# Linear attention and MLP on one core: finest level of the first two tiles by ScalarE and GpSimd, states by scans, no products of zeros in the first tile, and another order

## The chip, the cores and the metric

The kernel runs on one core of a Trainium2 chip. The metric is device time in microseconds (us), lower is better. All data is float32 except what is named otherwise. PE is the matrix engine (TensorE), PEld its weight loads, DVE VectorE, ACT ScalarE, POOL GpSimd, and SP SyncE, which issues most DMAs.

## The reference

```
state = 0                                   # B=4, H=8, S=768, D=48
for t in range(S):                          # linear attention with decay (RWKV6)
    cur   = outer(u * k[t], v[t])
    y[t]  = r[t] @ (state + cur)
    state = w[t][:, None] * state + outer(k[t], v[t])
x = y as (B*S = 3072 tokens, H*D = 384)
h = x @ w_in                                # 384 x 2048
g = 0.5 * h * (1 + erf(h / sqrt(2)))
out = g @ w_out                             # 2048 x 384
```

## The kernel before

**Tiles.** The work is cut into eight tiles, x = 0 to 7: four batches, two halves of T = 384 steps each. A tile has four pairs of heads (NP = 4), two heads of a pair lying on the two halves of the 128 partitions. The steps of a tile are cut into NC = 6 chunks of C = 64. Even tiles begin a batch with a state of zeros; odd tiles go on from the last state of the tile before.

**Attention of one tile.** Inside a chunk, the matrix of r times decay times k is built by levels. At level h (1, 2, 4, 8, 16, 32) PE multiplies r and k with the decays up to that distance in them (`products`, line 452), a part of the result is copied from PSUM into `a_sb`, and DVE multiplies r and k with the decays of the next level (lines 494 and 505). Tiles 0 and 1 do these six levels (`halves`); tiles 2 to 7 use a scheme of quarters. The copies of `halves` are masked DVE copies for h = 1, 2, 4, 8 (line 516) and plain ACT copies of blocks for h = 16 and 32 (line 513). The diagonal, with u in it, is a product of its own and one masked DVE copy (line 465). Then k is transposed (line 685, copied by ACT in line 687), PE makes each chunk's sum of k times v (`kv_ps`, line 711), and DVE chains the states of the six chunks: one `scalar_tensor_tensor` per chunk and pair (line 726), plus one copy per unit for the first chunk (line 731). PE adds up y inside the chunks (line 752) and y from the states (line 797), whose stationary operand is 64 contiguous columns of a state. DVE's `fence` (lines 762, 764) stands between the two groups of products. ACT and DVE copy y to `xT` (lines 804, 820), partly by way of `ysb` (line 823) and DMAs.

**MLP of one tile.** `mlp(x - 1)` is run on PE beside attention(x). Tile 0's MLP is plain (line 1059 first, h = x @ w_in in 128x384 steps); the later ones use sums of halves of the operands to save products (lines 929 and 1073, 128x192 steps). The gelu is on ACT (line 961 and its like). w_in and w_out come in 16 pieces that three ACT and two DVE instructions convert (lines 333, 334, 336; 345, 349) during tiles 0 and 1.

**Order.** Every engine runs its instructions in the order of the program. That order is written out by hand: `PLAN[x]` is a string, each character of which runs one step of a stream. In tile 0, `.` and `s` are two units of the attention (heads 0 to 3, heads 4 to 7), `l` loads and transforms, `c` the weight conversion, `f` the first steps of the next tile, `x` three products of zeros. In later tiles, `.` is the MLP of the tile before, `s` the attention, `f` the next tile's first steps.

**Products of zeros.** `keep_warm(n)` issues n matmuls of 128x512 bf16 zeros: 8 at the start, 2 behind each of 12 products of tile 0, and 6 ahead of the first MLP product.

**PSUM.** The products take pairs of banks; tiles 0 and 1 have three pairs, and two single banks serve the MLP.

Of the kernel before, what the change touches and what calls it, by code (L numbers as in the profile page):

```python
# [36 lines left out]
NC_SP = 8  # L37
HALFWAY = 2
PLAN = {
    0: "l.s....llsl.lssslslss.lc.l.slslls...ssss..lcs.s.s.l.ss..ss..sccs.c.s.llpssslw..cs.ffpcc",  # L40
    1: (
        "..ccswccc.csl.scscs.s.sccwsc.clccs.ccsccc.csc.lscclswwclc.scs.wcssw.ss.cclcsc.ccs.lclccsc."
        "ccclfccccccfccfcccccfccfccwf.ff......fw.sl.w.x.wx...x..x...xww"
    ),
    2: (
        "s.s.....ss....ssw.ws.wl.wsss.wws.s..lsl...lws.w..s.ww....s.s..l..sss.lssss....s..s..s.sls."
        "llsf.sf.fs..fl.xx.x.fxx"
    ),
    3: (
        "ls.ls....lss..ss.....ss..l.s.lsss.sss.s.s.s.ss..sss..sssssss....s.s..l...s..l.sslslsf.ffs."  # L50
        "..x.lx..xxx"
    ),
    4: (
        "lls.s.sss..s.l.........ssss.....sss.s.ss.s..s.sllss...s.s..l.sss.ss..s.ss...s..sslsll.s..f"
        ".sf.sf..ff..xx.xflxx"
    ),
    5: (
        "..ss...s..ssl....sls...s.sss..sss..sss.sls...sllss..sssss.s..l..s.s...s.slll..s.ssfsf.fsf."
        "....xxx.lxx"
    ),  # L60
    6: (
        "ss..sss...s.....s.sl..s...l.s.ssls.s.s..s..sssssl......ss.ssss.sl.sl...s.....ss..llsssl.f."
        "s.fsf.f.f.xx.l.xffxx"
    ),
    7: "....ss.s...s.s.s....s.sss..ss.ss.sss..s..sss..sssssss......s.s....s..ssss.s...x.x..xxx",
}


# [5 lines left out]
def kernel(  # L74
# [149 lines left out]
        for _ in range(n):  # L224
            nc.tensor.matmul(t, lhsT=zeros[:, 0:128], rhs=zeros, start=True, stop=True)

    keep_warm(8)


    masks = {h: const.tile([128, C // 2], U8, name=f"mask{h}") for h in LEVELS if h < 16}  # L230
# [122 lines left out]
    def attention(x, unit):  # L353
# [53 lines left out]
        for h in LEVELS:  # L407
            nb = n_u // (2 * h)
            t2 = tot[h].rearrange("p (n two) -> p n two", two=2)
            tot[2 * h] = tot_sb[:, at_tot:at_tot + nb]  # L410
            nc.vector.tensor_mul(tot[2 * h], t2[:, :, 0], t2[:, :, 1])
            at_tot += nb
            if x >= 2 and h == 2:
                yield
# [27 lines left out]
        else:  # L442
            yield

        def products(bs, right, width, rest=False):
            d = pair("d")
            n = 0
            for b in bs:
                for i in range(NI):
                    for g in range(2):  # L450
                        for p in range(2):
                            nc.tensor.matmul(d[half[p], g, n * width:(n + 1) * width],  # L452
                                             lhsT=kc[half[g], b, i, p], rhs=right(half[g], b, i, p),
                                             start=True, stop=True)
# [14 lines left out]
        def halves():  # L469

            for h in LEVELS:
                m = C // 2 // h
                if np_ < NPART:

                    d = products(range(np_), lambda z, b, i, p: rc[z, b, i, p], C, h == 1)
# [14 lines left out]
                rk = bass.AP(tensor=r2.tensor, offset=r2.offset, ap=[r2.ap[0], [n_u - h, 2]] + list(r2.ap[1:]))  # L490
                tt = bass.AP(tensor=t2.tensor, offset=t2.offset, ap=[t2.ap[0], [1, 2]] + list(t2.ap[1:]))

                def update(z, r2=r2, t2=t2, k2=k2, tk=tk):
                    nc.vector.tensor_mul(*((k2, k2, tk) if z is k else (r2, r2, t2)))

# [8 lines left out]
                else:  # L504
                    nc.vector.tensor_mul(rk, rk, tt)
                yield
                ah = at.rearrange("p g n (m two j) -> p g n m two j", two=2, j=h)[:, :, :, :, 1, :]
                if h >= 16:

                    for p in range(2):  # L510
                        for i in range(m):
                            s = slice(p * 64 + i * 2 * h, p * 64 + i * 2 * h + h)
                            nc.scalar.copy(out=ah[s, :, :, i], in_=d[s, :, :, i])
                else:
                    mask = masks[h].rearrange("p (m j) -> p m j", j=h).unsqueeze(1).unsqueeze(1)
                    nc.vector.copy_predicated(out=ah, mask=mask.to_broadcast(ah.shape), data=d)
                if h == 1:
# [183 lines left out]
        def vs(b, i, g):  # L701
            o = ((parts[b] * NI + i) * 2 + g) * D
            return loaded[x][1][:, o:o + G]

        kvs = []
        for b in range(np_):
            kv_ps = pair("kv_ps")
            for i in range(NI):
                for p in range(2):
                    for g in range(2):  # L710
                        nc.tensor.matmul(kv_ps[half[g], p, i * D:(i + 1) * D], lhsT=k_t(b, i, p, g),  # L711
                                         rhs=vs(b, i, g)[half[p], 0:D], start=True, stop=True)
            kvs.append(kv_ps[:, :, 0:NI * D].rearrange("p c (q i e) -> p q i c e", q=Q, e=D))
        yield

        stq = st[:, 0:NP * NC * D].rearrange("p (q c e) -> p q c e", q=NP, e=D)
        totq = tot[C].rearrange("p (q c) -> p q c", q=qs)
        stq = stq[:, q0:q0 + qs]
        if not first:
            b4 = before[:, 0:NP * NC * D].rearrange("p (q c e) -> p q c e", q=NP, e=D)[:, q0:q0 + qs]  # L720

        def chain_states(steps):
            for c in steps:
                if c or not first:
                    for q in range(qs):
                        nc.vector.scalar_tensor_tensor(out=stq[:, q, c], in0=stq[:, q, c - 1] if c else b4[:, q, NC - 1],  # L726
                                                       scalar=totq[:, q, c:c + 1], in1=kvs[q // Q][:, q % Q, c // 2, c % 2],
                                                       op0=ALU.mult, op1=ALU.add)
                else:
                    for b in range(np_):  # L730
                        nc.vector.tensor_copy(out=stq[:, b * Q:(b + 1) * Q, c], in_=kvs[b][:, :, 0, 0])


        def swap(b):
            return parts[b] % 2
# [29 lines left out]

        if x == 0:

            inside()
            yield
            for z in last_r:  # L770
                z()
            yield
            chain_states(range(NC - 1 + int(first)))
            yield
            fences()
            yield
        else:
            for c in range(0, NC, 2):
                chain_states(range(c, min(c + 2, NC - 1 + int(first))))
                if x > 1 and c + 2 < NC:  # L780
                    yield
            yield
            inside()
            fences()
            yield

        for i in range(NI):
            for p in range(2):
                for b in range(np_):
                    q, c3 = divmod(i, N3)  # L790
                    for g in range(2):
                        c = 2 * c3 + (p + g) % 2
                        src, c0 = (st, c - 1) if c else (before, NC - 1)
                        if src is None:
                            continue
                        o = ((parts[b] * Q + q) * NC + c0) * D
                        nc.tensor.matmul(ys[b][0][c % 2][half[g ^ swap(b)], i * C:(i + 1) * C],  # L797
                                         lhsT=src[half[g], o:o + G], rhs=rc[half[g], b, i, c % 2],
                                         start=False, stop=True, skip_group_check=True)
        if split:  # L800
            for c, copy in enumerate((nc.scalar.copy, nc.vector.tensor_copy)):
# [516 lines left out]
```

## Time and profile before

| | |
|---|---|
| time, median of 3 runs | 590.56 us (588.85 to 590.85) |
| the profiled execution | 589.61 us, of which span 587.8 us |
| PE busy | 571.1 us (97% of the span) |
| PEld busy | 521.4 us (89%) |
| DVE busy | 425.5 us (72%) |
| ACT busy | 291.2 us (50%) |
| POOL busy | 58.6 us (10%) |
| tile 0's attention | about 9.4 to 41.6 us |
| first MLP product | at 44.4 us |
| last PE instruction ends | at 584.9 us |

A group's line reads: line, engine, operation, output and inputs by the program's names, shapes, count, then busy time and mean duration, then the idle time before it and what ended it. In a timeline the first two numbers are the start and the duration in us; what stands in brackets is the engine's idle time ahead of it, and its releaser. One call of a float32 product stands in the records as two matmuls.

### The profile page before, as it was taken

Reading aid. Unit: us, or ns where it says so; the run is one execution under the profiler, and the core shown is the slowest. Engines: PE = TensorE matmul, PEld = TensorE weight load, DVE = VectorE, ACT = ScalarE, POOL = GpSimd, SP = SyncE. Lnnn points to the kernel's source line nnn. Section 1 sums busy time; section 2 is a strip of 40 time slices with the busy share of each in tenths; the row PEclk is TensorE's granted clock in tenths of the full one; section 3 lists DMA queues with packets and bytes.
Section 4 is the critical chain, followed back from the end, with each engine's and each line's share of the span. In section 5 each row is a group of like instructions: output and inputs, shape, how many; then the busy total and the mean of one; then the engine's idle time right before and its main releaser. Section 6 shows DMA issues by size and latency. Waiting matters only on the chain. (4 is left out here: it accounts for less than half of the span.)

```text
span 587.8 us, 17656 instructions
## 1 busy us (share of the span) xinstructions
PE 571.1 (97%) x7602; PEld 521.4 (89%) x7616; DVE 425.5 (72%) x825; ACT 291.2 (50%) x668; POOL 58.6 (10%) x63
## 2 busy tenths in 40 slices
PE   5789999999999999999999999999999999999997
PEld 3576666799999999999999999999998999999997
DVE  5988968989758975777959986777759987420332
ACT  2368898446362567235462467245561467335400
POOL 3100000013000130012000130002100111003100
PEclk8999999999999999999999999999999999999999
DMA  6749742253032542354122632344224333114201
GB/s 230 221 135 352 265 168 78 79 142 52 5 89 64 157 58 41 90 142 93 26 55 79 151 70 44 86 139 74 27 41 119 86 42 42 29 45 55 28 13 35
DMA packets 62430, 55.09 MB, mean 94 GB/s; under 512 B 32400, under 2 KB 47504, under 8 KB 62352
## 3 DMA queue, kind: packets, MB, share of 16 engines
q1 hardware_dynamic: 50832, 45.62, 25.5%
q0 software_dynamic: 11424, 8.26, 10.8%
q8 instruction: 60, 0.98, 0.7%
q14 instruction: 18, 0.15, 0.1%
q10 hardware_dynamic: 96, 0.07, 0.1%
HBM read 36.24 MB, written 4.72 MB: 70 GB/s over the span
## 5 line engine op out<-in xcount | busy, mean ns | idle before, releaser
L929 PE MATMUL h_ps<-xT,w_in_sb 128*128 128x192 f32 x560 | 111.5, 330 | 0.6 <-DVE o_sb L1196 0.6
L980 POOL DMA_DIRECT2D g<-o_sb x42 | 50.6, 1229 | 478.2 <-ACT o_sb L965 468.9
L929 PEld LDWEIGHTS h_ps<-xT,w_in_sb 128*128 128x128 f32 x560 | 93.0, 190 | 4.7 <-ACT g L961 1.6
L929 PE MATMUL u_ps<-s,w_in_sb 128*128 128x192 f32 x224 | 41.2, 327 | 0.0
L1073 PE MATMUL o_ps<-w_out_sb,g 128*128 128x192 f32 x224 | 39.8, 326 | 0.0
L929 PEld LDWEIGHTS u_ps<-s,w_in_sb 128*128 128x128 f32 x224 | 37.1, 190 | 0.2
L1073 PEld LDWEIGHTS o_ps<-w_out_sb,g 128*128 128x128 f32 x224 | 37.0, 190 | 0.0
L604 ACT COPY a_sb<-d 32x256 f32<-32x256 f32 (+8 forms) x90 | 32.6, 362 | 4.9 <-PE d L588 3.4
L1059 PE MATMUL h_ps<-xT,w_in_sb 128*128 128x384 f32 x96 | 33.2, 494 | 0.0
L452 PEld LDWEIGHTS d<-rkw 64*64 64x64 f32 x1152 | 19.4, 138 | 14.7 <-issue 10.5
L1073 PE MATMUL o_ps<-w_out_sb,f 128*128 128x192 f32 x176 | 32.0, 331 | 0.0
L1073 PE MATMUL o_ps<-t,g 128*128 128x192 f32 x176 | 31.4, 330 | 0.0
L1073 PE MATMUL o_ps<-t,s 128*128 128x192 f32 x176 | 31.2, 328 | 0.0
L1073 PE MATMUL o_ps<-t,e 128*128 128x192 f32 x176 | 30.6, 326 | 0.5 <-issue 0.5
L621 DVE COPY_PREDICATED a_sb<-quarter,d 128x480 f32<-128x480 uint8 (+5 forms) x54 | 23.2, 439 | 10.5 <-PE d L588 9.3
L726 DVE SCALAR_TENSOR_TENSOR st<-st,tot_sb,kv_ps 128x48 f32<-128x48 f32 x160 | 28.9, 258 | 2.6 <-PE kv_ps L711 2.5
L1073 PE MATMUL o_ps<-w_out_sb,e 128*128 128x192 f32 x176 | 30.7, 328 | 0.0
L982 DVE TENSOR_TENSOR g<-g,o_sb 128x384 f32<-128x384 f32 x14 | 7.6, 549 | 31.2 <-ACT o_sb L965 31.1
L1073 PEld LDWEIGHTS o_ps<-t,e 128*128 128x128 f32 x176 | 28.9, 190 | 0.7 <-issue 0.7
L1073 PEld LDWEIGHTS o_ps<-t,g 128*128 128x128 f32 x176 | 28.6, 190 | 0.5
L1073 PEld LDWEIGHTS o_ps<-w_out_sb,f 128*128 128x128 f32 x176 | 28.5, 190 | 0.6
L1073 PEld LDWEIGHTS o_ps<-t,s 128*128 128x128 f32 x176 | 28.8, 190 | 0.2
(163 smaller groups left out, 1171.3 us busy)
## 6 DMA issues: line engine op xcount, KB each, us to landing
rkw<-in_rkw_dram SPq DMA_DIRECT2D x54, 256.0 KB, 3.6
g<-o_sb POOLq DMA_DIRECT2D x42, 192.0 KB, 3.6
raw<-in_w_out_dram SPq DMA_DIRECT2D x8, 768.0 KB, 6.2
v_in<-in_v_dram SPq DMA_DIRECT2D x8, 584.0 KB, 4.6
raw<-in_w_in_dram SPq DMA_DIRECT2D x5, 768.0 KB, 7.5
out_dram<-o_sb SPq DMA_DIRECT2D x20, 192.0 KB, 2.0
rkw<-kx SPq DMA_DIRECT2D x72, 48.0 KB, 2.0
rkw<-in_rkw_dram SPq DMA_DIRECT2D x6, 384.0 KB, 6.2
```

The source lines that it names most:

```text
L452: nc.tensor.matmul(d[half[p], g, n * width:(n + 1) * width], lhsT=kc[half[g], b, i, p], rhs=right(half[g], b, i, p), start=True, stop=True)
L604: nc.scalar.copy(out=at[z, g, first:behind, (a + 1) * h:], in_=d[z, :, :, to] if g == slice(None) else d[z, :, to])
L621: nc.vector.copy_predicated(out=an[:, :, :, :, (a + 1) * h:], mask=mask.to_broadcast(data.shape), data=data)
L726: nc.vector.scalar_tensor_tensor(out=stq[:, q, c], in0=stq[:, q, c - 1] if c else b4[:, q, NC - 1], scalar=totq[:, q, c:c + 1], in1=kvs[q ...
L929: nc.tensor.matmul(o, lhsT=lhsT, rhs=rhs, start=start, stop=True, skip_group_check=True)
L980: nc.gpsimd.dma_start(out=g, in_=z, accum_op=ALU.add)
L982: nc.vector.tensor_add(g, g, z)
L1059: nc.tensor.matmul(h_ps, lhsT=w_in_sb[:, f // FI, j, f % FI * 128:(f % FI + 1) * 128], rhs=xT[:, j, :], start=(j == 0), stop=(j == NJ - 1))
L1073: nc.tensor.matmul(o, lhsT=lhs(j), rhs=rhs(j), start=start and j == 0, stop=(j == HF - 1), skip_group_check=True)
```

## The change

1. *Zeros.* `keep_warm(8)` at the start becomes `keep_warm(24)`, and the two behind each product of tile 0 go.
2. *Level 1 of tiles 0 and 1.* The mask of level 1 is not built. ACT copies the whole block of level 1 from PSUM, and GpSimd sets to zero what does not belong there, with one `affine_select` for each half of the partitions. The diagonal's copy on DVE comes behind them.
3. *States.* DVE makes the states of one unit in one `tensor_tensor_scan` over 48 x 2 x 6 elements of each partition, in which the chunk's index runs innermost. Its operands are written by ACT: the factors (the decay of a whole chunk, spread over 48 columns, zero at the first chunk) and what is added (k times v, out of PSUM). In odd tiles ACT first writes the last state of the tile before into the PSUM block of k times v, the other chunks' products are moved on by one, and the last chunk's isn't made. The states lie with the chunk innermost, so that a stationary operand of the products of line 797 is 48 columns, 12 elements apart, where it was 64 contiguous ones. The two buffers of states aren't zeroed on GpSimd any more.
4. *Order.* All strings of `PLAN` are new.

```diff
-    0: "l.s....llsl.lssslslss.lc.l.slslls...ssss..lcs.s.s.l.ss..ss..sccs.c.s.llpssslw..cs.ffpcc",
+    0: "..s..slll.ll..lssslllcsls.ls.pss.sc..ssss..l.ss.lss.sl.sls.s...cs.s.ccl.ssl..scwcs.fpccf",
...
-        "..ccswccc.csl.scscs.s.sccwsc.clccs.ccsccc.csc.lscclswwclc.scs.wcssw.ss.cclcsc.ccs.lclccsc."
+        ".sws.sccc.sc.c.scccssscccc.clscc.cwccslscc.s.scc.cssww.clcssc.scs.scccccs.clc.cwslcl.cccwc"
...
-    keep_warm(8)
+    keep_warm(24)
...
-    st_bufs = [const.tile([128, NP * NC * D + G - D], F32, name=f"st{i}") for i in range(2)]
-    for s in st_bufs:
-        nc.gpsimd.memset(s, 0.0)
+    st_bufs = [const.tile([128, NP * NC * D], F32, name=f"st{i}") for i in range(2)]
...
+    chain_tot = const.tile([128, 2, NP, NC], F32, name="chain_tot")
+    nc.gpsimd.memset(chain_tot, 0.0)
...
+            if 2 * h == C:
+                z0, z1 = (t2[:, :, z].rearrange("p (q c) -> p q c", q=qs) for z in range(2))
+                c0 = slice(1, NC) if first else slice(0, NC - 1)
+                nc.vector.tensor_mul(chain_tot[:, int(not first), q0:q0 + qs, 1:], z0[:, :, c0], z1[:, :, c0])
+                continue
...
+        def chain_factors():
+            for b in range(np_):
+                t = chain_tot[:, int(not first), parts[b] * Q:(parts[b] + 1) * Q].rearrange("p q c -> p (q c)")
+                nc.scalar.copy(out=factors(b).rearrange("p (e z) -> p e z", e=D), in_=t.unsqueeze(1).to_broadcast([128, D, Q * NC]))
...
-            if x == 0 and not rest:
-                keep_warm(2)
...
+                if h == 1:
+
+                    nc.scalar.copy(out=ah, in_=d)
+                    for z in half:
+                        a1 = ah[z, :, :, :, 0]
+                        nc.gpsimd.affine_select(out=a1, in_=a1, pattern=[[0, 2], [0, a1.shape[2]], [2, m]], base=1,
+                                                channel_multiplier=-1, compare_op=ALU.is_ge, fill=0.0)
...
+                    if x == 0 and h == 16:
+                        chain_factors()
...
-                else:
+                elif h > 1:
                     mask = masks[h].rearrange("p (m j) -> p m j", j=h).unsqueeze(1).unsqueeze(1)
...
             kv_ps = pair("kv_ps")
+            if late:
+                nc.scalar.copy(out=kv_ps[:, 0, 0:NI * D].rearrange("p (q i e) -> p q i e", q=Q, e=D)[:, :, 0],
+                               in_=states(before, b).rearrange("p (e q c) -> p q e c", q=Q, c=NC)[:, :, :, NC - 1])
             for i in range(NI):
                 for p in range(2):
+                    if late and p and i % N3 == N3 - 1:
+                        continue
+                    o = (i + (late and p)) * D
                     for g in range(2):
-                        nc.tensor.matmul(kv_ps[half[g], p, i * D:(i + 1) * D], lhsT=k_t(b, i, p, g),
+                        nc.tensor.matmul(kv_ps[half[g], p ^ late, o:o + D], lhsT=k_t(b, i, p, g),
                                          rhs=vs(b, i, g)[half[p], 0:D], start=True, stop=True)
...
-        def chain_states(steps):
-            for c in steps:
-                if c or not first:
-                    for q in range(qs):
-                        nc.vector.scalar_tensor_tensor(out=stq[:, q, c], in0=stq[:, q, c - 1] if c else b4[:, q, NC - 1],
-                                                       scalar=totq[:, q, c:c + 1], in1=kvs[q // Q][:, q % Q, c // 2, c % 2],
-                                                       op0=ALU.mult, op1=ALU.add)
...
+        def chain_added(b):
+            nc.scalar.copy(out=by_step(added(b)), in_=kvs[b][:, :, 0:NI * D].rearrange("p c (n e) -> p e n c", e=D))
+
+        def chain_states(b):
+            nc.vector.tensor_tensor_scan(out=states(st, b), data0=factors(b), data1=added(b), initial=0.0, op0=ALU.mult, op1=ALU.add)
...
-                        o = ((parts[b] * Q + q) * NC + c0) * D
-                        nc.tensor.matmul(ys[b][0][c % 2][half[g ^ swap(b)], i * C:(i + 1) * C],
-                                         lhsT=src[half[g], o:o + G], rhs=rc[half[g], b, i, c % 2],
+                        o = parts[b] * PART + q * NC + c - int(first)
+                        nc.tensor.matmul(ys[b][0][c % 2][(g ^ swap(b)) * G:(g ^ swap(b)) * G + D, i * C:(i + 1) * C],
+                                         lhsT=st[half[g], o:o + (D - 1) * Q * NC + 1:Q * NC], rhs=rc[half[g], b, i, c % 2],
```

More of the change, by code (lines that the diff above doesn't have):

```diff
@@ L225, in keep_warm @@
             nc.tensor.matmul(t, lhsT=zeros[:, 0:128], rhs=zeros, start=True, stop=True)
-    keep_warm(8)
-    masks = {h: const.tile([128, C // 2], U8, name=f"mask{h}") for h in LEVELS if h < 16}
+    keep_warm(24)
+    masks = {h: const.tile([128, C // 2], U8, name=f"mask{h}") if h > 1 else None for h in LEVELS if h < 16}
     masks[0] = const.tile([128, C], U8, name="mask0")
@@ L443, in attention, with factors, products @@
             yield
-        def products(bs, right, width, rest=False):
+        PART = Q * NC * D
+        def factors(b):
+            if x == 0:
+                return s_home[:, 0:PART] if parts[b] else kx[:, NP * T:NP * T + PART]
+            return kx[:, (NPART + b) * PART:(NPART + b + 1) * PART]
+        def chain_factors():
+            for b in range(np_):
+                t = chain_tot[:, int(not first), parts[b] * Q:(parts[b] + 1) * Q].rearrange("p q c -> p (q c)")
+                nc.scalar.copy(out=factors(b).rearrange("p (e z) -> p e z", e=D), in_=t.unsqueeze(1).to_broadcast([128, D, Q * NC]))
+        def products(bs, right, width):
             d = pair("d")
@@ L703, in vs, with states, by_step @@
             return loaded[x][1][:, o:o + G]
+        late = int(not first)
+        def states(buf, b):
+            return buf[:, parts[b] * PART:(parts[b] + 1) * PART]
+        def by_step(z):
+            return z.rearrange("p (e n c) -> p e n c", e=D, c=2)
         kvs = []
@@ L712, in attention @@
                                          rhs=vs(b, i, g)[half[p], 0:D], start=True, stop=True)
-            kvs.append(kv_ps[:, :, 0:NI * D].rearrange("p c (q i e) -> p q i c e", q=Q, e=D))
+            kvs.append(kv_ps)
+        if x > 1:
+            chain_factors()
         yield
[L716 to L720, printed above, removed]
@@ L722, in chain_states, with added @@
[L722 to L731 removed]
+        def added(b):
+            if x == 0:
+                return kx[:, parts[b] * Q * T:parts[b] * Q * T + PART]
+            return kx[:, b * PART:(b + 1) * PART]
@@ L766, in attention @@
         if x == 0:
+            for b in range(np_):
+                chain_added(b)
             inside()
@@ L772, in attention @@
             yield
-            chain_states(range(NC - 1 + int(first)))
+            for b in range(np_):
+                chain_states(b)
             yield
@@ L777, in attention @@
         else:
-            for c in range(0, NC, 2):
-                chain_states(range(c, min(c + 2, NC - 1 + int(first))))
-                if x > 1 and c + 2 < NC:
+            if x == 1:
+                chain_factors()
+            for b in range(np_):
+                chain_added(b)
+            if x > 1:
+                yield
+            for b in range(np_):
+                chain_states(b)
+                if x > 1 and b + 1 < np_:
                     yield
```

33 lines of the change are left out of this document (17 added, 16 removed).

## The prediction

> **What bounds the kernel now.** I first read the busy time of each engine by stretches of the span. The columns are the stretch, its length, then busy microseconds and (instructions) of PE, PEld, DVE, ACT and POOL, the granted clock, the DMA share and GB/s.
>
> ```profile
> 9.40:41.60 32.20, 26.25 (x972) 20.99 (x985) 26.30 (x72) 13.30 (x24) 2.88 (x5) 0.95 0.59 183
> 41.60:44.40 2.80, 2.75 (x104) 2.14 (x104) 2.69 (x5) 2.00 (x5) 0.00 (x0) 1.00 0.46 124
> 44.40:118.80 74.40, 74.35 (x1071) 49.64 (x1071) 64.57 (x107) 57.46 (x95) 0.00 (x0) 1.00 0.53 185
> 118.80:584.90 466.10, 464.13 (x5456) 447.57 (x5455) 326.03 (x614) 216.04 (x543) 50.64 (x42) 1.00 0.32 70
> ```
>
> From 44.4 us (the first MLP matmul) to 584.9 PE is idle for 2.0 us in all. So the time can move in three ways only: the first MLP matmul starts at another time; PE has more or less to do; PE gets new waits. PE's waits confirm that nothing large is left:
>
> ```profile
> PE d L452 <- DMA rkw<-in_rkw_dram: 3.5, 1, 3.5
> PE kv_ps L711 <- issue: 1.0, 1, 1.0
> PE h_ps L929 <- DVE o_sb L1196: 0.6, 2, 0.4
> PE y_ps L797 <- DVE fence L762: 0.5, 1, 0.5
> ```
>
> Then PE's timeline of tile 0, which the plan runs as two units (heads 0-3, heads 4-7):
>
> ```profile
> 2.29 3.59 PE L225 MATMUL warm<-zeros 128*128 128x512 bf16 x8 [2.29 <-ACT zeros L217]
> 9.43 1.56 PE L452 MATMUL d<-rkw 64*64 64x64 f32 x48 [3.55 <-DMA rkw<-in_rkw_dram]
> 28.09 0.93 PE L452 MATMUL d<-rkw 64*64 64x64 f32 x48
> 28.95 0.39 PE L225 MATMUL warm<-zeros 128*128 128x512 bf16 x1
> 29.48 0.93 PE L452 MATMUL d<-rkw 64*64 64x64 f32 x48
> 41.56 1.60 PE L452 MATMUL d<-rkw 64*64 64x32 f32 x96
> 44.40 1.78 PE L1059 MATMUL h_ps<-xT,w_in_sb 128*128 128x384 f32 x5
> ```
>
> A product takes 1.56 us at a granted clock of 0.50 (9.4 to 12.8 us) and 0.93 at full clock; with its zeros a product comes every 1.40 us (28.09 to 29.48), without them every 0.87. DVE runs beside it: 26.30 of 32.20 us, with a masked copy or update on nearly every step:
>
> ```profile
> 12.83 1.02 DVE L516 COPY_PREDICATED a_sb<-mask,d 128x384 f32<-128x384 uint8 x1
> 22.88 0.96 DVE L505 TENSOR_TENSOR rkw<-rkw,tot_sb 128x768 f32<-128x768 f32 x1 [0.47 <-PE d L452]
> 29.08 0.96 DVE L505 TENSOR_TENSOR rkw<-rkw,tot_sb 128x768 f32<-128x768 f32 x1 [0.44 <-PE d L452]
> 38.02 1.84 DVE L726 SCALAR_TENSOR_TENSOR st<-st,tot_sb,kv_ps 128x48 f32<-128x48 f32 x10
> ```
>
> **Part by part: tile 0.** *Level 1.* Two DVE copies of 1.02 go (2.04). In their place ACT copies 128x384 (0.48, the L823 row) and GpSimd makes two selects, after which alone DVE's diagonal copy may start. No row has a select on 64 partitions with 384 elements. The nearest is the identity's:
>
> ```profile
> masks.py:199 POOL TENSOR_SCALAR_AFFINE_SELECT ident<-ident 128x128 f32<-128x128 f32 x1 | 0.3, 295 | 0.1
> L289 POOL COPY rkw<-ident 32x128 f32<-32x128 f32 x4 | 2.4, 589 | 0.2
> ```
>
> Three times 0.295 is 0.89; with a fixed part of 0.1 (the smallest memsets take 0.093) it is 0.69. I take 0.85, the row being the same operation; the upper bound is three of the L289 copies, 1.77. By hand: products 9.45 to 10.4, ACT copy to 11.85, selects to 13.65, where DVE went on at 12.83 before, so it waits 0.9 more. Net: 0.9 - 2.04 = -1.15.
>
> *Levels 2 to 32.* Without zeros PE is ahead of DVE, and DVE's waits for products (0.47 and 0.44 above, 0.43 at 30.48) go; with about 0.3 from the reordered weight conversion, -1.65.
>
> *Zeros at the start.* 24 instead of 8: 8 cold at 0.449 to 5.9 us, 16 at 0.218 (the six at 43.09 took 1.31) to 9.4, just when the first product's load lands. Taken at nothing; if all 24 stay cold they end at 13.1 and the first products lose some 2.6, if the clock is up by 9.4 they gain up to 0.6 each.
>
> *States.* Per unit the ten steps (1.84) and the first copy (0.26) give way to one scan over 128x576 on DVE and ACT copies of factors and of the products (128x576, about 0.7 by the 0.80 of 128x768). No row shows a scan. Plain elementwise work would give 0.76 (between 0.555 for 384 and 0.958 for 768 elements), the slowest rows 1.34 (0.895 per 384); I take 1.05. DVE saves about 1.05 a unit, but ACT now sets the end: second weight conversion (2.94), factors, the level-16 and level-32 copies (1.4 and 0.95 per unit), two kt copies, two copies of products. I get the last copy of y that feeds the transposing DMA (39.57 before) 9.5 us after the last k update instead of 9.1: +0.4.
>
> Sum for tile 0: -1.15 - 1.65 + 0.4 = **-2.4** (first MLP matmul at 42.0 instead of 44.4), bounds -3.5 and +1.
>
> [...]
>
> **Tile 1.** Beside the MLP of tile 0, PE has no slack (74.35 of 74.40). Level 1 gets selects of twice the size, about 1.45 each; the diagonal copies land near 50.5, and the second piece of w_in, whose conversion DVE does behind them, is ready near 53.8 where PE wants it at 53.3: **+0.5** (0.3 to 1.0). The products of k and v wait for ACT's copy of the last state, which is queued behind a gelu that waits for PE's own preceding matmuls: **+0.8** (0 to 1). Other shifted waits, y against its fence above all: **+0.25**.
>
> **PE's work.** In the odd tiles the last chunk's k-v product is not made: 8 calls of 48, 16 records of 96 per tile (the row of 96 takes 1.61, so 16.6 ns each), four tiles: 64 x 16.6 ns = **-1.06**. The MLP and the products are the same in number. The state's products (704 records of L797) now load 48 columns at a stride of 48 bytes instead of 64 contiguous ones. The pitch of a record is 16.6 ns for 64, 48 and 32 moved columns alike, so something other than columns sets it: taken at nothing; bounds -1.1 (16 of 64 columns fewer, a tenth of it on the pitch) and +5 (7 ns a record).
>
> **Later tiles.** The planner's text changes in all, yet attention blocks stay within about 1.3 us of their place in the MLP's order; scans halve DVE's 3.7 us of state steps (two of 1.84), which nobody waited for (PE waited 0.3 for them). ACT gains two factor and two product copies a tile, some 2.8 us on an engine busy 46%. The last-state copy, queued on ACT in tiles 3, 5 and 7, costs tenths if nothing covers it; the MLP blocks of 1.3 to 3.9 us between steps do. Nothing, bounds -0.5 and +1.
>
> **Sum**: -2.4 - 1.06 + 0.5 + 0.8 + 0.25 = -1.9. The profiled execution took 589.61 (span 587.8 and 1.8 around it), the median is 590.56; the same shift gives 587.7 and **588.6**. 0.3%, about what a measurement can tell, is 1.8 us.
>
> **Rivals.**
>
> *Slower: GpSimd's selects are the new bound.* Where I took S = 0.85, tile 0 has four in a row ahead of the second diagonal copy (slack 0.3), and tile 1 four of double size, of which two stand ahead of PE: together 8 x (S - 0.85) - 0.3. From S = 1.1 on the whole gain is gone, from 1.35 it is slower by over 0.3%; S = 1.5 costs 4.9: 593.6. For it: the L289 copies (mean 0.589 for 128 elements of a strided view) and a view broken into rows. Against: the same operation at 0.295. Chance 0.16.
>
> *Slower: strided weights.* On a PE without slack every extra nanosecond of the 704 loads counts: 5.7 ns more are 4.0 us, 592.7. For it: DVE's 384 elements take 0.87 at 16 bytes' stride (L419) and 0.555 contiguous. Against: the constant pitch of 16.6 ns. [...] Chance 0.12.
>
> *No change.* The start is gained as worked out, but tile 1 takes it back: stalls at their upper bounds and without the zeros tile 0's clock drops in pauses (products 1.56 instead of 0.93; two on the path are 1.2). -1.9 + 0.5 + 0.2 + 1.2 = 0: 590.6. Chance 0.20.
>
> *More gain.* Start at its bound (-3.5), no stall in tile 1: -3.5 - 1.06 + 0.25 = -4.3: 586.3. Chance 0.12.
>
> **How the numbers follow.** Forecast 0.40. Of it 0.30 lies beyond 0.3%, 0.10 within. Faster: 0.30 + 0.12 = 0.42. Same: 0.10, 0.16 of no change, 0.02 of the strided weights = 0.28. Slower: 0.16 + 0.10 + 0.04 = 0.30. Range: from 585.4 (the greater gain with cheaper weight loads) to 594.6 (S near 1.6); outside remain the slowest selects and sums of bounds, under 2 in 10.
>
> **What would show it.** Right: the first MLP matmul at 41 to 43 us; selects of 0.7 to 1.0 on 384 elements; no zeros between products and a clock of 1.00 from 9.4; a scan of 0.8 to 1.35; 16 to 17 ns per record of the state's products; PE waits of 1 to 2 us between 50 and 90. Wrong: selects over 1.1, DVE or PE waiting for POOL in tile 1, clocks under 1 after 13 us, or the state's products above 1.8 us for 96.

## The result and the profile after

The changed kernel takes 598.61 us (median of 6 runs, 597.5 to 601.99); the kernel before takes 590.41 in the six runs with it. The ratio is 1.0154, interval 1.0131 to 1.0177: slower by 8.2 us by the medians and some 9 by the ratio, where 1.9 us less was forecast; the forecast's range ended at 594.6. The profiled execution took 598.14 us with a span of 596.4, 8.5 us more than the one of before (589.61).

Busy time by stretches, in the columns that the prediction names. The cuts are the first product of tile 0, about the end of its y, and the first MLP product, as before; the last cut lies elsewhere than before, so the last two rows are to be read together:

```profile
9.02:42.30 33.28, 23.27 (x959) 20.92 (x962) 23.04 (x51) 16.47 (x30) 5.57 (x9) 0.90 0.59 194
42.30:45.34 3.04, 2.99 (x108) 2.38 (x106) 2.83 (x5) 1.63 (x4) 0.00 (x0) 0.93 0.36 72
45.34:125.00 79.66, 78.22 (x1067) 52.61 (x1067) 62.95 (x91) 61.54 (x104) 1.99 (x2) 1.00 0.50 167
125.00:593.00 468.00, 466.57 (x5396) 450.66 (x5395) 317.82 (x496) 230.85 (x571) 50.71 (x42) 1.00 0.33 70
```

From the first MLP product to the last matmul's end it is 548.1 us (45.34 to 593.4), where before it was 540.4 (44.40 to 584.8). So 7.7 of the 8.5 us arise on a PE that is nearly always busy, and 0.9 at the start. The group of the state's products (those that add up y from the states) shows the first part. The numbers are durations in ns, least, median and most; the first line is of the kernel before, whose line 797 became 841:

```profile
L797 PEld LDWEIGHTS y_ps<-rkw,st x704: 129/135/135, 38.1 to 516.4; 64*64 64x64 f32 x176
```

```profile
L841 PEld LDWEIGHTS y_ps<-rkw,st x704: 171/199/203, 38.5 to 526.2; 64*48 64x48 f32 x176
L841 PE MATMUL y_ps<-rkw,st x704: 256/260/360, 38.5 to 526.3; 64*48 64x64 f32 x176
```

Loading 48 columns takes 199 ns where 64 took 135. PE's timeline has the groups of products, one for each tile. Two of before (tiles 1 and 2), then three of after (tiles 2 to 4):

```profile
102.27 1.63 PE L797 MATMUL y_ps<-rkw,st 64*64 64x64 f32 x96
181.65 1.46 PE L797 MATMUL y_ps<-rkw,st 64*64 64x64 f32 x80
```

```profile
184.18 2.25 PE L841 MATMUL y_ps<-rkw,st 64*48 64x64 f32 x80
250.48 2.66 PE L841 MATMUL y_ps<-rkw,st 64*48 64x64 f32 x96
321.14 2.25 PE L841 MATMUL y_ps<-rkw,st 64*48 64x64 f32 x80
```

Before, 96 records took 1.63 (once 1.70) and 80 took 1.40 to 1.46. Over tiles 1 to 7 that is 17.38 instead of 10.85 us: **+6.5 us**, 10.5 ns for each of 624 records. The second part is a wait, and the third a saving that didn't come (tiles 1 and 2 of after):

```profile
84.28 1.60 PE L752 MATMUL kv_ps<-v_in,kx 64*64 64x48 f32 x80 [1.37 <-ACT kv_ps L744]
176.78 1.61 PE L752 MATMUL kv_ps<-v_in,rkw 64*64 64x48 f32 x96
```

PE waits 1.37 us for ACT's copy of the last state, and the 80 products of k and v of an odd tile take as long as the 96 of an even one: nothing is saved. PE's idle time from the first MLP product on is 2.9 us where it was 2.0, so its other waits are 0.5 less; with 0.9 at the start, 0.9 + 6.5 + 1.4 - 0.5 = 8.3 of 8.5 us are placed.

The start: tile 0 reached level 2 sooner, as forecast, and lost it at the end. DVE's timeline, PE's timeline, and PE's granted clock (the column after the busy time) in two slices of 1 us:

```profile
15.75 0.96 DVE L531 TENSOR_TENSOR rkw<-rkw,tot_sb 128x768 f32<-128x768 f32 x1
...
20.01 0.96 DVE L531 TENSOR_TENSOR rkw<-rkw,tot_sb 128x768 f32<-128x768 f32 x1 [0.56 <-PE d L471]
...
28.67 0.56 DVE L520 TENSOR_TENSOR rkw<-rkw,tot_sb 128x384 f32<-128x384 f32 x1 [0.78 <-PE d L471]
```

```profile
35.65 0.30 PE L788 MATMUL y_ps<-a_sb,v_in 64*64 64x64 f32 x7
37.89 0.81 PE L788 MATMUL y_ps<-a_sb,v_in 64*64 64x64 f32 x41 [1.94 <-issue]
38.53 3.96 PE L841 MATMUL y_ps<-rkw,st 64*48 64x64 f32 x78
```

```profile
40.00:41.00 1.00, 1.00 (x30) 0.50 0.00 0
41.00:42.00 1.00, 1.00 (x24) 0.50 0.00 0
```

The first level-2 update starts at 15.75 (before 17.76) and the last k update of the leading unit at 28.67 (before 30.48), a lead of 1.8 us. Then PE stops for 1.94 us in the middle of a group, "issue", that is for nothing that the profile shows, where the kernel before stopped for 0.96; behind it the clock falls to 0.50, and the y from the states stretches over 4.1 us (38.53 to 42.60). At the same count of weight loads, the 732nd, PE was 1.4 us ahead; behind the stop it is 0.5 us late, and at the first MLP product 0.9. So of the 2.7 us lost, 1.0 is the longer stop; the rest lies before and behind it.

### The profile page after: what moved, and what is told of

Its sections match the earlier page's. It is cut to its first block, busy times and chain, and to the rows that moved or that the text cites. A ratio compares the mean times of both kernels' runs of the same rounds, so it can differ in the third digit from the quotient of the medians.

```text
span 596.4 us, 17427 instructions
## 1 busy us (share of the span) xinstructions
PE 578.1 (97%) x7542; PEld 529.3 (89%) x7544; DVE 412.4 (69%) x668; ACT 313.1 (52%) x711; POOL 61.4 (10%) x68
## 3 DMA queue, kind: packets, MB, share of 16 engines
q0 software_dynamic: 11424, 8.26, 10.6%
## 4 chain that ended last, share of the span: by engine, by line
PE 63%; DVE 3%; DMA 0%; SPq 0%; ACT 0%; issue 0%; DVEq 0%
PE o_ps L1117 27%; PE h_ps L973 14%; PE u_ps L973 13%; PE d L615 4%; PE y_ps L841 2%; PE y_ps L788 1%; PE kv_ps L752 1%; DVE rkw L426 1%; DVE kx L387 1%; DMA xT<-ysb 0%; PE d L606 0%; DVE rkw L380 0%; SPq L871 0%; DVE s L941 0%; PE u_ps L615 0%
## 5 line engine op out<-in xcount | busy, mean ns | idle before, releaser
L1103 PE MATMUL h_ps<-xT,w_in_sb 128*128 128x384 f32 x96 | 33.9, 497 | 0.0
L768 DVE TENSOR_TENSOR_SCAN st<-kx 128x576 f32<-128x576 f32 x15 | 19.6, 1345 | 15.8 <-ACT kx L765 15.8
L1016 ACT COPY u_ps<-h_ps 128x384 f32<-128x384 f32 x28 | 13.2, 472 | 30.9 <-PE h_ps L973 30.9
L1117 PEld LDWEIGHTS o_ps<-w_out_sb,e 128*128 128x128 f32 x176 | 28.7, 190 | 0.3
```

The source lines that it names most:

```text
L768: nc.vector.tensor_tensor_scan(out=states(st, b), data0=factors(b), data1=added(b), initial=0.0, op0=ALU.mult, op1=ALU.add)
L1016: nc.scalar.copy(out=u_of[q], in_=a_of[q])
L1103: nc.tensor.matmul(h_ps, lhsT=w_in_sb[:, f // FI, j, f % FI * 128:(f % FI + 1) * 128], rhs=xT[:, j, :], start=(j == 0), stop=(j == NJ - 1))
L1117: nc.tensor.matmul(o, lhsT=lhs(j), rhs=rhs(j), start=start and j == 0, stop=(j == HF - 1), skip_group_check=True)
```

## Experiments

Theory S: the stride of the weights costs most of it. Rivals: the tile of 48 columns costs it (C), or the new order and tile 1's waits do (P; later O for the order alone). A second theory, on the stop in tile 0, came up on the way (L). In labels, `a` and `ac` are made from the changed kernel, `b` from the kernel before; each profile is of one execution.

**1. The stride alone, and its size.** In the changed kernel only the addresses of the weights are moved. These kernels, and all `ac` ones, then read other values than the states, so their y isn't the reference's; the number and shape of the instructions stay:

```diff
-                        o = parts[b] * PART + q * NC + c - int(first)
+                        o = parts[b] * PART + (q * NC + c - int(first)) * 24
-                                         lhsT=st[half[g], o:o + (D - 1) * Q * NC + 1:Q * NC]
+                                         lhsT=st[half[g], o:o + D]
```

(`o:o + (D - 1) * 2 + 1:2` and the same with 4 in the other two.)

a_contig: 

> The changed kernel, but the state's products read 48 contiguous columns as weights where it reads 48 columns 48 bytes apart (the addresses are moved, so these weights are not the right states; number and shape of all instructions stay). Theory S (the stride costs): 96 records take 1.63 us again instead of 2.66, 80 take 1.40 instead of 2.25; 6.5 us over tiles 1 to 7 and 1 to 1.5 us in tile 0: about 590.5. Rival C (48 columns of 64, or the output on 48 partitions, cost the time): 2.66 stays, 598. Rival P (the new order and tile 1's waits are the greater part): 596 or more.

a_stride2: 

> As the run before, with columns 8 bytes apart. [...] If any stride costs the same: 2.66. If the cost grows evenly with the distance: little over 1.63.

a_stride4: 

> The same with columns 16 bytes apart. [...] If the cost grows evenly with the distance: about 1.9.

One group of 96 records in PE's timeline of each of the three, with columns 4, 8 and 16 bytes apart in that order:

```profile
384.39 1.56 PE L841 MATMUL y_ps<-rkw,st 64*48 64x64 f32 x96
```

```profile
521.04 1.56 PE L841 MATMUL y_ps<-rkw,st 64*48 64x64 f32 x96
```

```profile
388.08 2.40 PE L841 MATMUL y_ps<-rkw,st 64*48 64x64 f32 x96
```

At 4 and 8 bytes 1.56 us, at 16 bytes 2.40, at 48 bytes 2.66; a load takes 120, 121, 183 and 199 ns. C is out: a group of 96 records with 48 contiguous columns is 0.07 us cheaper than with 64. Columns 8 bytes apart cost a load 1 ns more than contiguous ones, columns 16 bytes apart 63 ns more, columns 48 bytes apart another 16. What lies behind the step between 8 and 16 bytes, and behind the 16 ns, no run here shows. The single runs of 8 and 16 bytes took 594.18 and 597.84 us.

The time of a_contig is 593.28 us (10 runs, 590.7 to 595.1) against 588.94 of the kernel before beside it, ratio 1.0068 (1.0045 to 1.0091): the stride is some 5 us of 9 by the ratios (6.3 by the two profiled executions), and about 4 are left.

**2. The other way round: the kernel before with that stride alone.**

```diff
-        stq = st[:, 0:NP * NC * D].rearrange("p (q c e) -> p q c e", q=NP, e=D)
+        stq = st[:, 0:NP * NC * D].rearrange("p (y e z c) -> p y z c e", y=NPART, z=Q, e=D)
```

(and the weights as in the changed kernel)

b_strided: 

> The kernel before, with its states stored with the chunk innermost by the same chain of DVE steps, so that alone the state's products change: 48 columns 48 bytes apart, output on 48 partitions. Theory S: 96 records take 2.66 us, 80 take 2.25; +6.5 us in tiles 1 to 7 and 1 to 1.5 in tile 0: about 598. Rival P: within 1 us of the kernel before, 590 to 591.

596.93 us, ratio 1.0115 (1.0082 to 1.0148); 96 records take 2.66, 80 take 2.31, and PE needs 546.8 us from the first MLP product on instead of 540.4. DVE's steps write at that stride too (291 ns each for 258), and PE waits 0.8 us for them once; nearly all of the rest is the weights. With the old order and no other change the greater part of the loss is there: P is out as the main cause, and S stands with its size.

**3. The zeros.** ac_zeros is a_contig with the old zeros; b_zeros is the kernel before with the new ones:

```diff
-    keep_warm(8)
+    keep_warm(24)
...
-            if x == 0 and not rest:
-                keep_warm(2)
```

ac_zeros: 

> The changed kernel with contiguous weights for the state's products (wrong states, as before) and with the zeros of the kernel before: 8 at the start, 2 behind each product of tile 0. Theory Z (without zeros PE's pauses in tile 0 let the clock fall to 0.50 for 4 us or more, somewhere after 18 us, and this holds the first MLP product back): the clock is 1.00 from 14 us on, the first MLP product comes at 43 to 44 instead of 45.4, and the time is 1 to 2.5 us less than with contiguous weights alone, with less spread. Rival Q (the zeros cost their 0.53 us a product, and the start is set by ACT and DVE): first MLP product at 45 to 47, time the same or up to 1.5 us more.

b_zeros: 

> The kernel before with the zeros alone changed: 24 at the start, none behind the products. Theory Z: a stretch of about 4 us at a clock of 0.50 somewhere in tile 0 after 18 us; the first MLP product within 1 us of 44.4 in spite of the freed PE, runs spread over 3 us or more. Rival Q (and the step of the prediction): DVE's waits for products go, first MLP product at 42.5 to 43, time -1.5.

ac_zeros took 594.4 us (ratio 1.0066, 1.0039 to 1.0093), no different from a_contig. The first MLP product came at 46.01, as rival Q had it, but behind a stop of 3.12 us where a_contig's was 1.68, so this profile doesn't tell what the zeros do to the start. b_zeros took 588.97 (0.9981, 0.9953 to 1.001): no difference that can be measured. In its profile the clock does fall to 0.50 twice (20 to 23 and 37 to 40 us), and the first MLP product comes at 44.96. So the zeros cost about what they save, as far as these times can tell.

**4. Level 1, and the order, each alone in the kernel before.** b_plan takes the strings of `PLAN` alone, b_select the new copy and selects; in b_select0 and b_select0_48 the conditions are `x == 0 and h == 1` and `x or h > 1`:

```diff
+                if h == 1:
+                    nc.scalar.copy(out=ah, in_=d)
+                    for z in half:
+                        a1 = ah[z, :, :, :, 0]
+                        nc.gpsimd.affine_select(out=a1, in_=a1, pattern=[[0, 2], [0, a1.shape[2]], [2, m]], base=1,
+                                                channel_multiplier=-1, compare_op=ALU.is_ge, fill=0.0)
...
-                else:
+                elif h > 1:
```

b_select: 

> The kernel before with level 1 of tiles 0 and 1 alone changed: ACT copies the block, GpSimd selects, no masked DVE copy of level 1. With selects of 0.59 us on 384 elements, the first updates behind the diagonals come 1 to 1.5 us sooner; but from 26 us on PE's products with their zeros set the pace, so the first MLP product comes 0.3 to 1 us sooner (43.4 to 44.1), and the time falls by as much: 588 to 588.6 by the runs of before beside it at 589. Rival: the selects or ACT's copy in tile 1 make PE wait, and the time is the same or 0.5 us more.

b_plan: 

> The kernel before with the new strings of the order alone. Theory O (the order was made for the other changes and costs without them): first MLP product 0 to 2 us later than 44.4, more waits in tile 1, +1 to +3 us. Rival (the order is good by itself): -1 to -2 us. It also tells whether the waits of 1 us before the products of k and v in tile 1 come from the order or from ACT's copy of the last state.

b_select took 594.3 us (1.0093, 1.0064 to 1.0122) though its first MLP product came at 42.33. In tile 1, under the old order, PE waits for ACT's level-1 copy, and the clock falls behind the wait; in this profile, of the fastest of the 7 runs (591.08), the two cover the 3.6 us that PE takes longer than before from the first MLP product to its end:

```profile
54.48 1.60 PE L452 MATMUL d<-rkw 64*64 64x32 f32 x96 [2.23 <-ACT a_sb L495]
56.02 5.80 PE L1066 MATMUL h_ps<-xT,w_in_sb 128*128 128x384 f32 x12
```

```profile
56.00:57.00 1.00, 1.00 (x10) 0.50 1.04 407
```

b_plan took 598.73 us (1.0154, 1.0109 to 1.0199): the new order puts y close behind k and v, and with the old chain of states PE waits 5.8 us in four pieces for DVE's line 726. So the order belongs to the scans, and this run says nothing on its worth with them. b_select0 keeps the new level 1 to tile 0; b_select0_48 adds 48 contiguous columns:

b_select0: 

> The kernel before with ACT's copy and GpSimd's selects for level 1 in tile 0 only; tile 1 keeps its masked copy. Theory T (the selects gain the start 2 us, and the loss of the run with both tiles came from PE's wait of 2.2 us for ACT's copy in tile 1 and the halved clock after it): first MLP product at 42.0 to 42.8, no PE wait over 0.6 us in tile 1, -1.5 to -2.2 us against the kernel before. Rival: the earlier start runs into loads that aren't there sooner, tile 1 waits for them, and less than 1 us is left.

b_select0_48: 

> As the run before it, and the state's products read 48 contiguous columns where they read 64 (output on 48 partitions): 96 records take 1.56 us instead of 1.63, 0.5 us over tiles 1 to 7. About -2 to -2.7 us against the kernel before, below both kernels. Rival: no difference to the run before it.

590.52 us (1.0006, 0.9986 to 1.0026) and 589.49 (1.0002, 0.9981 to 1.0023): no difference, both expectations missed. Tile 0's program is the same in b_select, b_select0 and b_select0_48 up to the weights, yet the first MLP product came at 42.33, 46.79 and 43.38. So one execution can differ from another by 4 us there: the profile of b_select0 is of one of its longest runs (592.04), that of b_select0_48 of its shortest (587.71). What differs most is the stop in tile 0.

**5. The stop in tile 0.** In every profile of this case PE stops at the same place of its program, at its 859th or 860th weight load, whatever product stands there. Other stops, most of them shorter, lie near the 222nd, 350th, 478th and 606th, about 128 loads and 128 matmuls apart. The profile's queue "instruction" moves one packet (0.98 MB in 60, so 16 KB) for each such stretch. I read this, by the queue's name, as the loading of PE's code; no run here shows what is in the packets or what asks for them. The table has the time of the 732nd weight load, the start of the packet that follows, the stop at the 860th, the clock behind it, and the first MLP product (us):

| kernel | 732nd | packet | stop | clock behind | first MLP |
|---|---|---|---|---|---|
| before | 34.1 | 35.1 | 0.96 | 1.00 | 44.40 |
| b_select | 32.2 | 33.1 | 1.01 | 1.00 | 42.33 |
| b_select0_48 | 32.8 | 33.5 | 1.26 | 1.00 | 43.38 |
| b_select0 | 33.9 | 35.9 | 1.99 | 0.50 | 46.79 |
| after | 32.7 | 35.6 | 1.94 | 0.50 | 45.34 |
| a_contig | 34.1 | 36.6 | 1.68 | 1.00 | 45.45 |
| ac_zeros | 32.9 | 36.9 | 3.12 | 1.00 | 46.01 |
| ac_early | 34.5 | 36.0 | 1.67 | 1.00 | 46.05 |
| ac_late | 32.0 | 35.8 | 2.84 | 0.50 | 45.31 |
| ac_late2 | 32.4 | 33.8 | 0.80 | 1.00 | 42.86 |
| b_defer | 35.0 | 35.8 | 0.99 | 1.00 | 45.36 |

From the 732nd load to the first MLP product it is 10.1 to 10.6 us in the rows with a stop of 1.3 us or less, and 11.4 to 13.4 in the others.

Theory L: the packet waits for loads of weights in flight. ac_early and ac_late move two loads in the order of tile 0 (the two `l`: 16 steps sooner in ac_early, to the end in ac_late), ac_late2 one more. The lines are those of ac_late2:

```diff
-    0: "..s..slll.ll..lssslllcsls.ls.pss.sc..ssss..l.ss.lss.sl.sls.s...cs.s.ccl.ssl..scwcs.fpccf",
+    0: "..s..slll.ll..lssslllcsls.ls.pss.sc..ssss..l.ss.lss.sl.sls.s...cs.s.cc.ss..scwcs.llfpccf",
...
-        for _ in weight_in(i + 3):
-            pass
+        for j in () if i == 0 else (3, 4) if i == 1 else (i + 3,):
+            for _ in weight_in(j):
+                pass
```

ac_early: 

> The changed kernel with contiguous weights (wrong states), and the last two loads of a w_in piece in tile 0 issued 16 steps sooner in the order. Theory L (PE stands still at its 860th weight load, until a block of its code has come behind those loads): the stop there falls from 1.5-2 us to 1 us or less, the first MLP product comes by as much sooner, 44.5 instead of 45.4, time -0.5 to -1. Rival: the stop isn't about loads and stays at 1.5 to 3 us.

ac_late: 

> The changed kernel with contiguous weights (wrong states), and the last two loads of a w_in piece in tile 0 issued after the unit's y steps instead of before them. Theory L (PE's stop at its 860th weight load is a block of its code that waits behind those 0.5 MB of loads; a stop of 2 us or more also halves the clock for the next 3 us): DMA engines under 0.6 busy at the stop, stop 1.0 us or less, first MLP product at 44 to 44.8 instead of 45.4 to 46. The piece lands later, and tile 1 may wait up to 2 us for it, so the time may stay at 592 to 594. Rival: the stop stays at 1.5 to 3 us whatever is loaded.

ac_late2: 

> As the run with the two loads issued later, and a third load (the whole next piece of w_in, 0.75 MB) also issued later. In the runs so far PE's block of code is asked for when PE passes its 732nd weight load, its packet starts only when the loads in flight have drained (0.7 to 3.7 us after), and PE goes on 2.4 to 2.6 us behind the packet's start. Theory L in this form: with the DMA engines idle by then the packet starts within 1 us, and PE's stop at the 860th weight load is 1.2 us or less instead of 2.8. Rival (the start of the packet has nothing to do with the loads): it starts 2 us or more after that point again, and the stop is 1.7 us or more. Tile 1 waits longer for the pieces, so the time itself says nothing: 596 or more.

ac_early (593.57 us): stop 1.67, no gain. Its DMA engines were still 0.8 busy or more until 38.5 us; the packet started 1.5 us after the 732nd load all the same, but took 2.2 us itself, where the others took 0.9 to 1.4. ac_late (596.89 us) missed too: stop 2.84, most of it with the DMA engines idle. But the loads issued up to 31.6 us were in flight until 35.5, and the packet started at 35.8. ac_late2, one execution without the last of those loads, is the test; PE's timeline:

```profile
36.41 0.81 PE L789 MATMUL y_ps<-a_sb,v_in 64*64 64x64 f32 x41 [0.80 <-issue]
...
42.86 2.10 PE L1104 MATMUL h_ps<-xT,w_in_sb 128*128 128x384 f32 x6
```

The packet starts 1.4 us after the 732nd load instead of 3.9, the stop is 0.80, the clock stays at 1.00, and the first MLP product comes at 42.86: 0.9 us from the prediction's 42.0. Against a_contig that is 2.6 us sooner, of which 1.7 are there at the 732nd load already. (Its time is 595.17 us; in tile 1 PE waits 2.4 us for the late pieces.) So L in its second form, that the packet starts when the loads in flight have drained, came out in its one test. ac_early's packet, which started among busy engines, doesn't fit it; that loads in flight make the stop longer, by a later start or a slower packet, fits all of them and isn't shown beyond that.

**What halves the clock.** A longer stop doesn't always halve it: 1.94 us did in the changed kernel, 3.12 in ac_zeros didn't. The traces show what went with it. In all 19 profiles the granted clock changes only at borders that lie 3.41 us apart, or a whole multiple of that. Cut there, PE's rows stand so around the stop, first of after, then of ac_zeros (stretch, its length, PE's busy time, then the clock):

```profile
35.90:39.31 3.41, 1.47 (x61) 1.00 0.34 108
39.31:42.72 3.41, 3.41 (x86) 0.50 0.02 4
```

```profile
33.81:37.22 3.41, 2.25 (x100) 1.00 0.86 279
37.22:40.64 3.42, 1.42 (x73) 1.00 0.35 100
40.64:44.05 3.41, 2.96 (x131) 1.00 0.11 24
```

The stop of after lies whole in one stretch, 1.94 us idle; that of ac_zeros is shared out, 1.16 and 2.00 us idle. Over all stretches at full clock in the 19 profiles, the next stretch was halved in 14 of 14 cases with PE idle for 2.05 us or more in sum, in 19 of 24 from 1.6 to 2.05, and in none of some 3100 below. So pauses add up within a stretch: one of a_contig with 1.92 us idle in pauses under 1 us each was followed by half clock. What decides between 1.6 and 2.05 is open.

b_defer takes b_select0_48 and issues one load later:

```diff
-        for _ in weight_in(i + 3):
+        for _ in weight_in(i + 3) if i else ():
...
-                "l": chain(weight_in(0, True), islice(second, 5), weight_in(1, True), second, weight_in(2, True)),
+                "l": chain(weight_in(0, True), islice(second, 5), weight_in(1, True), second, weight_in(2, True), weight_in(3)),
```

b_defer: 

> The kernel before with level 1 of tile 0 by ACT and GpSimd, 48 contiguous weight columns for the state's products, and the load of the fourth piece of w_in (0.75 MB) issued after tile 0's y steps instead of 5 us before PE asks for its block of code. Theory L: PE's stop at the 860th weight load under 1 us in the profiled run, first MLP product at 42 to 43.2, no halved clock between 34 and 42 us; 586.5 to 588.5, -1.5 to -2.5 us against the kernel before, with less spread. Rival: the piece then comes too late for tile 1, which takes it back: no difference.

589.44 us, 0.9996 (0.9985 to 1.0006): no gain. In its profile the stop at the 859th load is 0.99 us, as theory L had it, but an earlier one (350th load) took 1.8 us with a clock of 0.50 behind it, and the start is 45.36. No version run here beats the kernel before by more than its interval.

**6. The products of k and v, and the order once more.** ac_kv and ac_kv2 are a_contig with the copy of the last state on DVE, and share the 80 records otherwise between the two halves of the partitions that the products read (halves of the array's rows, in the expectations); the list is ac_kv2's (sum, its half, the half it is read from). ac_plan is a_contig with the old `PLAN`.

```diff
-                nc.scalar.copy(out=kv_ps[:, 0, 0:NI * D]
+                for z in range(2):
+                    nc.vector.tensor_copy(out=kv_ps[:, z, 0:NI * D]
...
+            if late:
+                ones = [(0, 0, 1), (0, 1, 1), (1, 1, 1), (3, 1, 1), (4, 1, 1)]
+                calls = [c for n in range(5) for c in (ones[n], (n + 1, 0, 0))]
```

ac_kv: 

> The changed kernel with contiguous weights (wrong states), with DVE in place of ACT for the copy of the last state into PSUM, and in odd tiles two of six sums per unit read from the other half of the partitions (wrong sums), so that both halves of the array's rows get 40 of the 80 records instead of 48 and 32. Theory K (48 records on one half take as long as 96 on both): 80 records take 1.33 us instead of 1.60. The wait of 1.1 us ahead of the products of k and v in tile 1 goes if ACT's queue behind the gelu is its cause: time -1 to -1.5 in all. Rival: the pitch has another cause and stays at 1.60; or the wait moves to DVE's queue and stays over 0.8.

ac_kv2: 

> As the run with sums moved to the other half, which had moved two sums of a unit and so only swapped 48 and 32: now one of six per unit is moved, and the calls alternate between the halves, 40 records each (wrong sums; DVE in place of ACT for the copy of the last state). Theory K (a half of the array's rows takes one record per 33 ns): 80 records in 1.33 us instead of 1.60. Rival: 1.60 again, whatever the halves get.

PE's wait of 1.1 to 1.4 us before the products of tile 1 is gone in both, so the copy in ACT's queue was its cause; the time doesn't show it (593.39 us, 1.0062, 1.0037 to 1.0086 for ac_kv; ac_kv2's single run took 591.16). ac_kv had moved twice as many sums as meant, 48 and 32 with the halves swapped, and took 1.60 again. With 40 and 40 alternating, in tile 3:

```profile
239.99 1.46 PE L754 MATMUL kv_ps<-v_in,rkw 64*64 64x48 f32 x80
```

1.46 instead of 1.60, not 1.33, and 1.45 and 1.46 in tiles 5 and 7, but 1.62 in tile 1. So the split, or the order that changed with it, matters in three of four tiles; that the fuller half sets the time is not shown.

ac_plan: 

> The changed kernel with contiguous weights (wrong states), and the order of the kernel before in all tiles. Theory O (what is left of the loss without the stride, 3 to 4 us, is the new order: its loads on PE's stop in tile 0, its place for the products of k and v in tile 1): stop at the 860th weight load about 1 us, first MLP product at 42.5 to 44.5; in tile 1 the wait of 2 us for ACT's level-1 copy, as in the run of level 1 alone; about 591. Rival (ACT's further copies and GpSimd's selects cost it under any order): 593 or more.

604.11 us (three runs, 602.3 to 608.93; 1.0249, 1.0177 to 1.0321), and a fourth of 612.34: the old order doesn't suit the new steps. The profile is of the fourth and explains it alone: PE waits 2.9 us for ACT's level-1 copy, 3.7 for its copy of the last state and 5.2 for fences.

Theory O falls, since the new order is the better one for the new steps. Of the 4 us that a_contig is behind, its profile (591.8 us, 2.2 over before's) has 1.05 at the start and 1.15 at ACT's copy of the last state. The rest lies in runs that weren't profiled. Their granted clocks point one way: 0.993 in the mean over a_contig's ten runs, 0.999 over the 13 of before beside them. By a profile's measure (one halved stretch of 3.41 us in 590 is 0.003) that is an estimate of two halved stretches more in a run, each worth 1.7 us at most; which pauses bring them stays open.

## Why the prediction was wrong, step by step

- **The state's products, "taken at nothing": the step that failed.** It was argued that the pitch of 16.6 ns (time from record to record) is the same for 64, 48 and 32 moved columns, so something other than columns sets it. Those rows vary the moved operand and say nothing on reading weights. The run with 16 bytes' stride shows 25 ns a record, the change's 48 bytes 27.7, the contiguous 48 columns 16.3. The rival of strided weights named the cause, at 4.0 us and a chance of 0.12; it measured 6.5 in tiles 1 to 7, above the bound of 5. The prediction's own sign of being wrong, over 1.8 us for 96, came at 2.66.
- **Start, -2.4: +0.9 measured, at its bound of +1.** Its three terms came out so:
  - Level 1: -2.0 (forecast -1.15). The first product began 0.4 sooner and at full clock, and a select took 0.59 and not 0.85. The 0.4 is no gain of the change: in kernels with the old zeros the first product began anywhere from 8.2 to 9.4.
  - Levels 2 to 32: +0.2 (forecast -1.65). DVE's waits for products did not go: they are 1.8 us in sum up to the last k update, where the kernel before had 1.3. Without zeros between, PE was idle for 2.17 us of the stretch up to 18.8, and the clock was 0.50 from there to 22.2.
  - From the last k update to the copy of y that feeds the DMA: +3.1 (forecast +0.4). About 1.0 is PE's longer stop, listed among before's waits as 0.96 us of "issue" and not asked about; about 1.0 is the first half of y from the states, at half clock and with strided weights; the rest lies ahead of the stop. In ac_late2, with a stop of 0.80, full clock and contiguous weights, the start is 42.9.
- **Zeros:** the 24 at the start ended at 9.1 (forecast 9.4) and the first products ran at full clock (0.93 us, where the first of before took 1.56); the clock fell later, in pauses, as the rival of no change said.
- **k and v, -1.06: 0.** The number of records was multiplied by a mean pitch, but 80 records, 48 on one half of the partitions and 32 on the other, took as long as 96. How they are shared and ordered matters (1.46 in ac_kv2, in three tiles); what sets it is open.
- **Tile 1:** the wait for the last state was 1.4 for 0.8; no PE wait behind the selects (forecast 0.5), which took 0.99 on 768 elements.
- **Scan:** 1.35 us for 576 elements, where 1.05 was taken:

```profile
L768 DVE TENSOR_TENSOR_SCAN st<-kx x15: 1331/1351/1359, 36.8 to 518.2; 128x576 f32<-128x576 f32 x15
```

PE's waits name the scan nowhere.

## What to carry to other kernels

Before storing a matrix for another engine's sake, ask how PE will read it: weight loads of 48 columns that lie 16 and 48 bytes apart cost 9 and 11 ns a record more than contiguous ones here, on an engine without slack. A row that varies one operand says nothing on the other. A count of matmuls was no time here: the 80 of k and v, shared 48 and 32 between the two halves of the partitions, took 1.60 us, and 96 took 1.61. An "issue" wait at a fixed place of the program is worth a question, since what is in flight beside it may make it longer (0.80 us in ac_late2, 2.84 in ac_late). And whether PE's pauses cost clock was read here from what was idle in sum over 3.41 us, not from the longest pause.

## What wasn't expected of the hardware

- Weight loads of 48 columns: 120 ns contiguous, 121 at 8 bytes, 183 at 16, 199 at 48 bytes.
- PE goes on 2.3 to 2.9 us after the start of a packet read as code (3.6 in ac_early), and the packet started 0.8 to 4.0 us after the 732nd load.
- The clock was halved behind 3.41 us stretches with 1.6 us of idle PE or more in sum (19 of 24 up to 2.05 us, 14 of 14 from there on), and for 3.41 us or a multiple.
- A select on 64 partitions with 384 elements took 0.59 us, with 768 elements 0.99.
